# Feed-forward tiles of 512 rows instead of 256, with 512-column first products, in a fused attention and two-feed-forward kernel

## The chip, the cores and the metric

One NeuronCore of a Trainium2 chip runs the whole program. The metric is the device time of one execution in microseconds (us). TensorE (PE) does the matrix products, VectorE (DVE), ScalarE (ACT) and GpSimd (POOL) the elementwise work, and SyncE (SP) issues most transfers.

## The reference

Eight batches of an attention without softmax, with a squared ReLU, feed a feed-forward layer of eight experts (top 1, with rows that skip it), and then a shared feed-forward layer whose activation is a rational function.

```python
# u, v: (8, 3072, 256); z: (8, 3072, 64)
scores = (1 / S) * z @ z.T
x = u * (np.maximum(scores, 0) ** 2 @ v)            # 24576 rows of 256
# experts: w1 (8, 256, 1024), w2 (8, 1024, 256)
do = x @ w_skip > 0
e = argmax(x[do] @ w_gate); gate = softmax(...)[e]
x[do] += gate * (np.maximum(x[do] @ w1[e], 0) @ w2[e])
# shared: w_in (256, 2048), w_out (2048, 256)
h = x @ w_in
g = (a0 + a1*h + a2*h**2 + a3*h**3) / (1 + abs(b0)*abs(h) + abs(b1)*h**2 + 1e-6)
out = g @ w_out
```

## The kernel before

Every product is made three times in the type fp32r, from operands split into a high and a low part (high by high, high by low, low by high).

**Attention** is cut into 1152 *ticks*, each of 256 query rows by 256 key rows: four score products (`S`, L649 and L650, from `T1` and its swapped copy `T4`), ReLU and square on ACT (L653, L656), a split into `ah` (ACT or DVE) and `al` (DVE, L664), and twelve products with `V` into the PSUM bank `accA` (L672). Twelve ticks make a row tile, which is then gated with `u` (`xs`, L731), routed to its expert and scattered to DRAM.

**Feed-forward** work is cut into *tiles* of 256 gathered rows (`mr`), transposed by PE (`mt`, L1090) and split into `mx` (L1095, L1098). A tile runs through *units*, four for an expert tile (kind 1) and eight for a shared tile (kind 2). A unit covers 256 columns of the hidden layer: twelve first products of 256 columns (`h`, L1054, in two halves `l1a` and `l1b`), the activation, and twelve second products (`l2h`, `l2l`, L1065) which add up in the PSUM bank `accM`. The activation of a shared unit is a chain over three engines: `abs` and `p1` on ACT (L1202, L1203), `q0` (L1209) and `q1` (L394), `p2`, `p3` on DVE (L1215, L1216), `ln`, `ex` on ACT (L1217, L1218), `gh`, `v`, `w` on DVE (L1219, L1220, L1222), `gl` (L394). For `q0`, `q1`, `gl` and some splits the planner chooses between DVE, POOL and ACT. After the last unit `mo` takes the sum out of `accM` (ACT, L1117, or DVE, L1112).

**Order.** Batches form five groups of 1, 2, 2, 2, 1. Expert units of a group are followed by its shared units; the attention of the following groups is mixed into the shared units (these stretches are called mixed below). `CARRY` = 1 tile of each group is put off to the next group's shared units. After the last tick come 56 shared units with the last group's 32 expert units (called `n`), and then the last group's 96 shared units alone. The class `Flow` simulates the engines with fixed costs and writes out one order for each engine; `PAR`, `SLIP` and `AHEAD` are its tuned due times and margins. `RINGS` gives the number of buffers of each tile name: of the eight PSUM banks six are called `b` (scores, `h`, transposes; `h` is given back by `w`, `S` by `al`), one is `accA`, one `accM`.

Of the kernel before, what the change touches and what calls it, by code (L numbers as in the profile page):

```python
# [8 lines left out]
F32 = mybir.dt.float32  # L9
F32R = mybir.dt.float32r  # L10
# [38 lines left out]
    "u.a": 4.46, "u.s": 22.81, "u.t": -51.57, "v.x": -18.1, "v.y": -44.71, "w.x": -20.81, "w.y": -12.53, "wsc.w": -0.79,  # L49
    "wsc1.f": 13.53, "wscc.w": -13.79, "wsch.w": -24.06, "wscl.w": 14.97,  # L50
# [3 lines left out]
SLIP = {"P": 7.64, "A": 0.24, "D": 0.96, "G": 27.68, "Q": 9.0}  # L54
# [15 lines left out]
class Flow:  # L70
# [7 lines left out]
    AHEAD = {"P": 35.26, "A": 5.17, "D": 97.38, "G": 8.79, "Q": 0.0}  # L78
# [138 lines left out]
def tile_attn_moe_moe2(  # L217
# [42 lines left out]

    NCH1 = E * FP1
# [10 lines left out]
    ident = sb.tile([P, P], F32, tag="mp", name="ident", bufs=3)  # L272
# [7 lines left out]
    onef = sb.tile([P, P], F32, tag="mu", name="onef", bufs=3)  # L280
# [3 lines left out]
    trif = sb.tile([P, P], F32, tag="mu", name="trif", bufs=3)  # L284
# [73 lines left out]
    def w_raw(n, wa, wb, fp):  # L358

        wide = wa.dtype != F32  # L360
        if wide:
            da = sb.tile([P, 512, 2], I32, tag="W", name=f"wda{n}", bufs=NW)
            db = sb.tile([P, 512, 2], I32, tag="W", name=f"wdb{n}", bufs=NW)
            wa, wb = wa.bitcast(I32), wb.bitcast(I32)
            la, lb, cw = da.rearrange("p c w -> p (c w)"), db.rearrange("p c w -> p (c w)"), 2
        else:
            da = sb.tile([P, 512], F32, tag="wr", name=f"wra{n}", bufs=WR)
            db = sb.tile([P, 512], F32, tag="wr", name=f"wrb{n}", bufs=WR)
            la, lb, cw = da, db, 1
        w_load(la, lb, wa, wb, fp, cw)  # L370
        return da, db

    def w_parts(n, dst, half, raw):
        o = 512 * half
        if raw.dtype == I32:
            r = sb.tile([P, 512], F32, tag="wr", name=f"wr{n}_{half}", bufs=WR)
            for _ in from_f64(r, raw, f"{n}_{half}"):
                pass
            raw = r
# [24 lines left out]
    def tl(tag, name, dt=F32, cols=512):  # L404
        return sb.tile([P, cols], dt, tag=tag, name=name, bufs=RINGS[tag])
# [29 lines left out]
    def put_unit(m, fp, kd):  # L435
        wn = ("v", m.w0 + fp) if kd == "n" else m.w0 + fp
# [9 lines left out]
    def m_tiles(kind, tls, nfp, base, nb):  # L446
        out = []
        for i, (g, idx) in enumerate(tls):
            m = MTile()
            m.kind, m.g, m.idx, m.nfp = kind, g, idx, nfp  # L450
            m.prev = out[-1][0] if out else None
            m.src = (xs_d, x2_d)[kind - 1][g][idx * TT : (idx + 1) * TT, :]
            m.w0 = base + (i // nb) * FP1 if kind == 1 else base
            out += [(m, fp) for fp in range(nfp)]
# [5 lines left out]
    own = [[(g, i) for i in range(nb * NIC)] for g, nb in enumerate(groups)]  # L460
# [7 lines left out]
    for g, nb in enumerate(groups):  # L468
        final = g == NG - 1 and g > 0
        if not final:  # L470
            us = m_tiles(1, [(g, i) for i in range(E * nb)], FP1, base, nb)
# [951 lines left out]
```

## Time and profile before

| | |
|---|---|
| median of 3 runs | 5650.31 us (5645.02 to 5654.39) |
| profiled execution | 5656.78 us |
| its span, first to last instruction | 5654.9 us |
| PE busy | 5462.3 us, 97% |
| DVE busy | 4607.6 us, 81% |
| ACT busy | 4177.9 us, 74% |
| POOL busy | 3151.3 us, 56% |
| granted TensorE clock, mean | 0.993 |

The shares are means over stretches with different limits, so the stretches have to be read apart. Busy time is the time in which at least one instruction of the engine was under way; PE's products overlap (one starts while the one before it drains), so their spacing is read from starts, not from durations.

### The profile page before, as it was taken

To read this page: it belongs to the slowest core of one execution; us is meant where nothing else is said; L and a number is where in the kernel's file an instruction comes from. 1 tells how busy PE (TensorE), PEld (TensorE's weight loads), DVE (VectorE), ACT (ScalarE), POOL (GpSimd) and SP (SyncE) were. 2 spreads that over 40 slices of the span, in tenths; PEclk is the share of its full clock that TensorE was granted. 3 is DMA by queue.
4 is the path that set the end of the run, shared out by engine and by line. 5 is a ranking of instruction groups with operands and counts; after the bars stand their busy time and mean duration, and the time that the engine had idled before them with its cause. 6 is when DMAs were issued, how large, how long until landed. Compare 5 with 4: busy or idle time off the path is not lost.

```text
span 5654.9 us, 119372 instructions
## 1 busy us (share of the span) xinstructions
PE 5462.3 (97%) x45285; PEld 5421.0 (96%) x45285; DVE 4607.6 (81%) x7474; ACT 4177.9 (74%) x7625; POOL 3151.3 (56%) x4456
## 2 busy tenths in 40 slices
PE   9999999999999999999999999999999999999887
PEld 9989999999999999999999999999999999999887
DVE  6765777776379899989539999899837999999999
ACT  8865888886278888888538878888826777765787
POOL 3443455444255565556326666666625777665787
PEclk9999999999999999999999999999999999999999
DMA  4376111114521110011451010001353000035000
GB/s 126 121 261 246 37 44 45 34 37 147 204 72 31 33 54 30 31 31 53 152 207 37 29 53 29 29 26 37 105 188 117 22 26 24 23 123 168 20 20 15
DMA packets 219786, 435.95 MB, mean 77 GB/s; under 512 B 30078, under 2 KB 145257, under 8 KB 197698
## 3 DMA queue, kind: packets, MB, share of 16 engines
q1 hardware_dynamic: 191938, 360.52, 18.9%
q0 software_dynamic: 27264, 67.71, 3.5%
q8 instruction: 358, 5.87, 0.4%
q14 instruction: 226, 1.85, 0.1%
HBM read 291.65 MB, written 153.09 MB: 79 GB/s over the span
## 4 chain that ended last, share of the span: by engine, by line
PE 73%; DVE 14%; issue 5%; POOL 3%; ACT 2%; DMA 2%; DVEq 0%; SPq 0%; POOLq 0%; ACTq 0%
PE accA L672 25%; PE h L1054 18%; PE accM L1065 18%; PE S L649 4%; PE S L650 4%; DVE mq L1220 3%; DVE mgh L1219 2%; DVE mq L1222 2%; DVE mp L1215 2%; POOL mgl L394 1%; DVE h L1216 1%; PE lp L761 1%; DMA wr<-in_moe_w_dram 1%; PE mt L1090 1%; PE xp L747 1%
## 5 line engine op out<-in xcount | busy, mean ns | idle before, releaser
L1054 PE MATMUL h<-mx,W 128*128 128x256 f32 x11904 | 1632.6, 284 | 48.7 <-DVE mq L1222 39.7
L1054 PEld LDWEIGHTS h<-mx,W 128*128 128x128 f32 x11904 | 1510.3, 189 | 59.1 <-issue 23.6
L672 PE MATMUL accA<-V,ah 128*128 128x256 f32 x9216 | 1293.4, 283 | 5.9 <-DVE xs L731 4.2
L394 POOL TENSOR_TENSOR mgl<-mq,mu 128x512 fp32r<-128x512 f32 x645 | 860.7, 1336 | 632.7 <-DVE mq L1222 436.3
L672 PEld LDWEIGHTS accA<-V,ah 128*128 128x128 f32 x9216 | 1182.8, 190 | 7.9 <-DVE xs L731 3.3
L1065 PE MATMUL accM<-W,mgh 128*128 128x256 f32 x7936 | 1125.5, 285 | 36.5 <-ACT mo L1117 19.6
L1065 PEld LDWEIGHTS accM<-W,mgh 128*128 128x128 f32 x7936 | 1025.7, 192 | 44.6 <-ACT mo L1117 24.3
L664 DVE TENSOR_TENSOR al<-S,ah 128x512 fp32r<-128x512 f32 x1152 | 784.8, 682 | 141.9 <-ACT ah L398 127.8
L653 ACT ACTIVATE S<-S 128x512 f32<-128x512 f32 x1152 | 676.0, 587 | 115.8 <-PE S L650 110.3
L1209 POOL TENSOR_SCALAR mq<-mu,coef 128x512 f32<-128x512 f32 x536 | 477.2, 890 | 505.7 <-ACT mu L1202 496.8
L672 PE MATMUL accA<-V,al 128*128 128x256 f32 x4608 | 746.0, 284 | 2.4 <-DVE al L664 2.3
L1202 ACT ACTIVATE mu<-h 128x512 f32<-128x512 f32 x768 | 458.2, 597 | 380.6 <-PE h L1054 271.1
L656 ACT ACTIVATE S<-S 128x512 f32<-128x512 f32 x1152 | 677.3, 588 | 21.9
L1215 DVE TENSOR_TENSOR mp<-mp,h 128x512 f32<-128x512 f32 x768 | 521.3, 679 | 194.6 <-ACT mp L1203 179.1
L1220 DVE SCALAR_TENSOR_TENSOR mq<-mq,mgh 128x512 f32<-128x512 f32 x768 | 671.7, 875 | 10.1
L1065 PE MATMUL accM<-W,mgl 128*128 128x256 f32 x3968 | 647.1, 285 | 30.5 <-POOL mgl L394 26.6
L1217 ACT ACTIVATE mu<-mq 128x512 f32<-128x512 f32 x768 | 484.8, 631 | 227.6 <-POOL mq L394 141.7
L672 PEld LDWEIGHTS accA<-V,al 128*128 128x128 f32 x4608 | 633.2, 191 | 3.4 <-DVE al L664 3.4
L1219 DVE SCALAR_TENSOR_TENSOR mgh<-h,coef,mu 128x512 fp32r<-128x512 f32 x768 | 570.4, 743 | 69.5 <-ACT mu L1218 56.2
L398 ACT ACTIVATE ah<-S 128x512 fp32r<-128x512 f32 x946 | 563.5, 596 | 71.6 <-PE accA L672 57.7
L394 POOL TENSOR_TENSOR mq<-mq,mu 128x512 f32<-128x512 f32 x422 | 562.9, 1334 | 59.0 <-DVE mq L1209 23.6
L650 PE MATMUL S<-T,T 128*128 128x256 f32 x2304 | 593.5, 282 | 0.0
(152 smaller groups left out, 8374.7 us busy)
## 6 DMA issues: line engine op xcount, KB each, us to landing
W<-wsc SPq DMA_DIRECT2D x96, 1024.0 KB, 6.1
wsc<-W SPq DMA_DIRECT2D x32, 1024.0 KB, 8.6
W<-wsc POOLq DMA_DIRECT2D x32, 1024.0 KB, 5.3
Wv<-wsc SPq DMA_DIRECT2D x64, 512.0 KB, 4.7
vr<-in_v_dram SPq DMA_DIRECT2D x96, 256.0 KB, 3.3
xs<-in_u_dram SPq DMA_DIRECT2D x96, 256.0 KB, 2.9
x<-xs SPq DMA_DIRECT2D x96, 256.0 KB, 2.2
mr<-x SPq DMA_DIRECT2D x96, 256.0 KB, 3.3
```

The source lines that it names most:

```text
L394: (nc.vector if e == "D" else nc.gpsimd).tensor_tensor(*a, **k)
L398: act(out, in_, AF.Copy)
L650: mm(o, lhsT=lw, rhs=T4[b, ic], start=False, stop=(jj == 1), skip_group_check=True)
L653: act(st["s"], st["s"], AF.Relu, scale=1.0 / S)
L656: act(st["s"], st["s"], AF.Square)
L664: ttt(st["lo"], st["s"], st["hi"].bitcast(F32), op=ALU.subtract)
L672: mm(accs[b, ic][:, it * TT : (it + 1) * TT], lhsT=a[:, jj * TT + it * P : jj * TT + (it + 1) * P], rhs=VV[b, jp][:, vi, jj * D : (jj + 1) ...
L1054: mm(o, lhsT=lw, rhs=rw, start=(ff == 0 and k == 0 and i == 0), stop=(ff == 1 and k == NK - 1 and i == 2), skip_group_check=True,)
L1065: mm(acc[:, it * TT : (it + 1) * TT], lhsT=(gh, gl)[part][:, c0 : c0 + P], rhs=w[i][:, 512 + ff * D : 512 + (ff + 1) * D], start=(first an ...
L1215: pt("p2", "D.602", ["p1", "abs"], lambda: ttt(s["p"], s["p"], s["h"], op=ALU.mult))
L1219: pt("gh", "D.663", ["ex", "p3"], lambda: stt(buf("mgh", F32R), s["h"], a0, s["u"], op0=ALU.add, op1=ALU.mult), ["mgh"])
L1220: pt("v", "D.602s", ["gh"], lambda: stt(s["q"], s["q"], CQ, s["gh"].bitcast(F32), op0=ALU.add, op1=ALU.mult))
```

## The change

1. **Tiles of 512 rows** (`m_tiles` with `nh` = 2, `plan_half`) for the experts of groups 2 to 4 and for all shared work; the experts of the first and the last group stay at 256. A unit now covers 128 hidden columns of 512 rows: six first products of 512 columns (`mm_l1w`), an activation of the same 128x512 size as before, and twelve second products of 256 columns (`mm_l2w`), six into each of two banks. A tile has twice the units of before, and the number of units stays the same (256 expert units and 768 shared ones). `CARRY` still counts tiles, so that 16 units are put off where 8 were.
2. **Buffers.** `accM` has two banks and `b` five; `mp` goes from 3 to 2 buffers, `T1` from 7 to 6, `mr` from 3 to 4 (of which a tile takes two), `mo` from 1 to 2; `zr` and `xt` now share the ring `wr`; the default rows (`dflt`) are kept in DRAM.
3. **Spacers** of 64 bytes stand before six tile names. In the built program tiles start at these bytes modulo 128. Before: `T1`, `T4`, `V`, `ah`, `al` 64; `W`, `mgh`, `mgl` 0; `mx` 96. Now: `T1`, `V`, `W` 32; `T4`, `ah`, `al`, `mgh`, `mgl`, `mx` 96. The moving and the stationary operand of nearly every product (not of `T1` by `T1`) are 64 bytes apart.
4. **Other due times and margins**, so that the planner writes another order.

```diff
 PAR = {
-    "S.a": 4.89, "S.t": -2.78, "T1.a": -21.74, "T1.s": 3.66, "T1.t": -47.54, "T1hi.a": -75.61, "T1hi.s": -3.79,
...
+    "S.a": 5.12, "S.t": -3.04, "T1.a": -59.25, "T1.s": -0.83, "T1.t": -58.86, "T1hi.a": -74.61, "T1hi.s": -18.49,
...
-SLIP = {"P": 7.64, "A": 0.24, "D": 0.96, "G": 27.68, "Q": 9.0}
+SLIP = {"P": 8.95, "A": 0.25, "D": 24.11, "G": 5.02, "Q": 9.0}
...
-    AHEAD = {"P": 35.26, "A": 5.17, "D": 97.38, "G": 8.79, "Q": 0.0}
+    AHEAD = {"P": 10.76, "A": 4.45, "D": 125.36, "G": 8.71, "Q": 0.0}
...
+    spacers = {"T4": 16, "V": 16, "ah": 16, "W": 16, "mgh": 16, "mx": 16}
+
+    def sbt(shape, dt, tag, **kw):
+        if tag in spacers:
+            sb.tile([P, spacers.pop(tag)], F32, tag="sp" + tag, name="sp" + tag, bufs=1)
+        return sb.tile(shape, dt, tag=tag, **kw)
...
-        "b": 6, "accA": 1, "accM": 1, "ah": 2, "al": 2, "V": NJP, "T1": NZC + 1, "T4": 2,
-        "zr": 1, "xt": 1, "xs": 2, "wr": WR, "W": NW, "mu": 3, "mp": 3, "mq": 3, "mgh": 3, "mgl": 3,
-        "mr": 3, "mx": 2, "mti": 4, "mo": 1,
+        "b": 5, "accA": 1, "accM": 2, "ah": 2, "al": 2, "V": NJP, "T1": NZC, "T4": 2,
+        "xs": 2, "wr": WR, "W": NW, "mu": 3, "mp": 2, "mq": 3, "mgh": 3, "mgl": 3,
+        "mr": 4, "mx": 2, "mti": 4, "mo": 2,
...
-    own = [[(g, i) for i in range(nb * NIC)] for g, nb in enumerate(groups)]
+    own = [[(g, i) for i in range(nb * NIC // 2)] for g, nb in enumerate(groups)]
...
-        us = m_tiles(2, t2s[g], FP2, base - (FP2 if final else 0), nb)
+        us = m_tiles(2, t2s[g], FP2, base - (FP2 if final else 0), 2)
...
+    def mm_l1w(h, w, xh, xl, ff, k):
+
+        c0 = k * TT + ff * P
+        xhk, xlk = xh[:, k * 512 : (k + 1) * 512], xl[:, k * 512 : (k + 1) * 512]
+        wh, wl = w[0][:, c0 : c0 + P], w[1][:, c0 : c0 + P]
+        for i, (lw, rw) in enumerate(((wh, xhk), (wh, xlk), (wl, xhk))):
+            mm(h, lhsT=lw, rhs=rw, start=(k == 0 and i == 0), stop=(k == NK - 1 and i == 2), skip_group_check=True)
+
...
+    def mm_l2w(accs_, w, ff, gh, gl, first, last, part):
+        for it in range(4):
+            for i in (0, 1) if part == 0 else (0,):
+                mm(
+                    accs_[it // 2][:, it % 2 * TT : (it % 2 + 1) * TT], lhsT=(gh, gl)[part][:, it * P : (it + 1) * P],
...
-        return "accA" if m.g == NG - 1 > 0 and (m.kind == 1 or m.idx % 2) else "accM"
+        return "accA" if m.g == NG - 1 > 0 and m.kind == 1 else "accM"
...
-        add(at["l1a"], ("l1a", t), "P.714", lambda: l1(0), after=prev + [("m", m.mi, "lo"), ("W", wn)], takes=[hu])
...
+        pl1 = "P.714" if m.nh == 1 else "P.69"
```

On PE, in a mixed stretch (the fourth batch's attention), first the order before: the first products of shared unit 218, and the second products of earlier units of the same weights' ring.

```order
L672 MATMUL accA3_7_25668<-V3_1_18718,al517_25624 128x256 x4
L1065 MATMUL accM38_25106<-W79_22959,mgh215_25562 128x256 x8
L1054 MATMUL h218_25734<-mx39_25408,W74_22542 128x256 x12
L1065 MATMUL accM38_25106<-W79_22959,mgl215_25613 128x256 x4
```

At the like place the changed program has this.

```order
L684 MATMUL accA3_8_24888<-V3_8_18530,al536_25287 128x256 x4
L1095 MATMUL accM23_0_24320<-W78_22082,mgh220_25225 128x256 x4
L1095 MATMUL accM23_1_24321<-W78_22082,mgh220_25225 128x256 x4
L1095 MATMUL accM23_0_24320<-W78_22082,mgl220_25260 128x256 x2
L1095 MATMUL accM23_1_24321<-W78_22082,mgl220_25260 128x256 x2
L1077 MATMUL h222_25360<-mx23_23910,W79_22281 128x512 x6
```

Twelve first products of 256 columns have become six of 512; the second products are as many and as wide as before, and go to two banks.

On PE, at the change from one shared tile to the next in the last group, the order before (tile 156 has `accM`, tile 157 the bank `accA`, whose buffer is free there; the program's name for both is `accM`):

```order
L1065 MATMUL accM156_78307<-W159_62330,mgh999_78608 128x256 x8
L1054 MATMUL h1004_78656<-mx157_78327,W156_62109 128x256 x12
L1065 MATMUL accM157_78677<-W152_61810,mgh1000_78674 128x256 x8
L1065 MATMUL accM156_78307<-W159_62330,mgl999_78671 128x256 x4
L1054 MATMUL h1005_78706<-mx157_78327,W157_62127 128x256 x12
```

and now, from tile 85 to tile 86:

```order
L1095 MATMUL accM85_0_72082<-W159_58214,mgl991_72660 128x256 x2
L1095 MATMUL accM85_1_72083<-W159_58214,mgl991_72660 128x256 x2
L1095 MATMUL accM86_0_72685<-W152_57472,mgh992_72663 128x256 x4
L1095 MATMUL accM86_1_72686<-W152_57472,mgh992_72663 128x256 x4
L1077 MATMUL h997_72699<-mx86_72222,W154_57652 128x512 x6
```

The new tile's second products used to start before the old tile's had ended, in another bank; now they stand right behind them and need both of its banks emptied first. Such a place comes half as often.

## Rows read from the trace of the kernel before

**Rows 1.** Windows: span, busy us (x count) of each engine, granted clock, DMA share, GB/s.

```profile
core 0: us, PE busy (x) PEld busy (x) DVE busy (x) ACT busy (x) POOL busy (x), PEclk, DMA share, GB/s
330.00:540.00 210.00, 183.61 (x1415) 180.15 (x1414) 112.56 (x198) 112.79 (x214) 64.82 (x120) 0.92 0.78 290
540.00:4270.00 3730.00, 3698.33 (x31052) 3688.41 (x31052) 2932.74 (x4879) 2760.38 (x5134) 1978.11 (x3037) 1.00 0.21 70
4270.00:5000.00 730.00, 691.24 (x5695) 684.43 (x5694) 704.19 (x1062) 555.12 (x981) 507.33 (x583) 0.99 0.12 38
5000.00:5290.00 290.00, 270.26 (x2192) 265.86 (x2192) 272.44 (x377) 179.16 (x295) 167.90 (x161) 0.98 0.41 136
5290.00:5655.00 365.00, 297.31 (x2274) 281.73 (x2272) 351.24 (x491) 291.43 (x453) 292.55 (x221) 0.97 0.06 17
```

**Rows 2.** Windows: the second and third mixed stretch.

```profile
1560.00:2720.00 1160.00, 1152.36 (x9695) 1150.96 (x9694) 1041.74 (x1717) 962.38 (x1787) 682.32 (x988) 1.00 0.13 42
2930.00:4050.00 1120.00, 1107.91 (x9289) 1102.12 (x9288) 1014.33 (x1649) 906.74 (x1669) 709.68 (x978) 1.00 0.13 42
```

**Rows 3.** Waits of PE, 540 to 4270: us in total, times, longest us.

```profile
PE S L649 <- DVE mq L1222: 4.8, 4, 1.4
...
PE h L1054 <- DVE al L664: 3.2, 3, 1.2
```

**Rows 4.** Waits of PE, 4270 to 5000, largest two.

```profile
PE xp L747 <- DVE xs L731: 18.1, 9, 2.2
PE accM L1065 <- ACT mo L1117: 15.7, 13, 1.7
```

**Rows 5.** Waits of PE, 5290 to 5655, the largest.

```profile
PE h L1054 <- DVE mq L1222: 37.1, 39, 1.6
```

**Rows 6.** Windows of line L1054 alone (PE, PEld).

```profile
540.00:4270.00 3730.00, 1077.92 (x7827) 992.58 (x7827) 1.00 0.21 70
```

**Rows 7.** The chain that ended last: start us, us, what.

```profile
1157.17 4.31 PE accA L672 x36
...
1576.40 4.32 PE h L1054 x36
```

**Rows 8.** Timeline of PE near 314: start us, us, what.

```profile
314.68 0.46 PE L570 MATMUL tp<-ident_r,zh 128*128 128x128 f32 x4
314.98 0.35 PE L649 MATMUL S<-T,T 128*128 128x256 f32 x1
```

**Rows 9.** Timeline of PE near 2976.

```profile
2976.13 1.11 PE L672 MATMUL accA<-V,ah 128*128 128x256 f32 x8
2977.07 0.64 PE L672 MATMUL accA<-V,al 128*128 128x256 f32 x4
```

**Rows 10.** Lines of DVE, 4270 to 5000: count | busy us, mean ns | idle before.

```profile
L1220 DVE SCALAR_TENSOR_TENSOR mq<-mq,mgh 128x512 f32<-128x512 f32 x146 | 143.9, 986 | 0.8
L1216 DVE SCALAR_TENSOR_TENSOR h<-mp,coef,h 128x512 f32<-128x512 f32 x147 | 108.6, 744 | 0.6
L1222 DVE SCALAR_TENSOR_TENSOR mq<-h,coef,mq 128x512 f32<-128x512 f32 x146 | 108.3, 742 | 1.5
L1219 DVE SCALAR_TENSOR_TENSOR mgh<-h,coef,mu 128x512 fp32r<-128x512 f32 x146 | 107.9, 739 | 0.0
L1215 DVE TENSOR_TENSOR mp<-mp,h 128x512 f32<-128x512 f32 x147 | 99.2, 675 | 0.5 <-ACT mp L1203 0.5
...
L394 DVE TENSOR_TENSOR mq<-mq,mu 128x512 f32<-128x512 f32 x45 | 33.5, 744 | 0.7
L394 DVE TENSOR_TENSOR mgl<-mq,mu 128x512 fp32r<-128x512 f32 x28 | 30.7, 1097 | 1.1
```

**Rows 11.** Lines of ACT, whole span.

```profile
L1117 ACT ACTIVATE mo<-accM 128x512 f32<-128x512 f32 x96 | 57.2, 595 | 20.8 <-PE accM L1065 19.5 <-DVE mq L1220 0.8
```

More of the change, by code (lines that the diff above doesn't have):

```diff
@@ L375, in w_parts @@
         if raw.dtype == I32:
-            r = sb.tile([P, 512], F32, tag="wr", name=f"wr{n}_{half}", bufs=WR)
+            r = sbt([P, 512], F32, tag="wr", name=f"wr{n}_{half}", bufs=WR)
             for _ in from_f64(r, raw, f"{n}_{half}"):
@@ L504, in tile_attn_moe_moe2 @@
             done, nt, span = len(x_tick), NA - len(x_tick), len(us) - POST
-            ms = m_tiles(1, [(NG - 1, i) for i in range(E * groups[-1])], FP1, 0, groups[-1])
-            lo, hi = span + TAIL, len(us) - CARRY * FP2
+            ms = m_tiles(1, [(NG - 1, i) for i in range(E)], FP1, 0, 1)
+            lo, hi = span + TAIL, len(us) - CARRY * 2 * FP2
             k = 0
@@ L629, in load @@
             b, ic = row // NIC, row % NIC
-            ut[row] = sb.tile([P, 2, RW], F32, tag="xs", name=f"xs{row}", bufs=RINGS["xs"])
+            ut[row] = sbt([P, 2, RW], F32, tag="xs", name=f"xs{row}", bufs=RINGS["xs"])
             nc.sync.dma_start(out=ut[row][:, :, 0:D], in_=rows4(u[b], 0, ic))
@@ L743, in r1 @@
             xp = R["xp"] = bank("b", f"xp{nm}")
+            R["xt"] = tl("wr", f"xt{nm}")
             for t in range(2):
@@ L752, in r2 @@
         def r2():
-            R["xt"] = sb.tile([P, 512], F32, tag="xt", name=f"xt{nm}", bufs=1)
             act(R["xt"], R["xp"], AF.Copy)
@@ L975, in load @@
             if v:
-                wt_t[n] = [sb.tile([P, 1024], F32R, tag="V", name=f"Wv{i}_{c}", bufs=NJP) for i in range(2)]
+                wt_t[n] = [sbt([P, 1024], F32R, tag="V", name=f"Wv{i}_{c}", bufs=NJP) for i in range(2)]
                 for i in range(2):
@@ L1070, in mm_l2, with plan_half @@
                         )
+    def mm_l2w(accs_, w, ff, gh, gl, first, last, part):
[3 more added lines that the diff above has]
+                    accs_[it // 2][:, it % 2 * TT : (it % 2 + 1) * TT], lhsT=(gh, gl)[part][:, it * P : (it + 1) * P],
+                    rhs=w[i][:, 512 + ff * D : 512 + (ff + 1) * D],
+                    start=(first and part == 0 and it % 2 + i == 0),
+                    stop=(last and part == 1 and it % 2 == 1), skip_group_check=True,
+                )
     def acc_tag(m):
-        return "accA" if m.g == NG - 1 > 0 and (m.kind == 1 or m.idx % 2) else "accM"
+        return "accA" if m.g == NG - 1 > 0 and m.kind == 1 else "accM"
     def plan_tile(m):
+        for h in range(m.nh):
+            plan_half(m, h)
+    def plan_half(m, h):
         mi = m.mi
-        k = ("m", mi)
+        k = ("m", mi, h)
+        st = {}
+        end = m.nh - 1
         def load():
-            m.rows = sb.tile([P, 2, RW], F32, tag="mr", name=f"mr{mi}", bufs=RINGS["mr"])
+            m.rows[h] = sbt([P, 2, RW], F32, tag="mr", name=f"mr{mi}_{h}", bufs=RINGS["mr"])
             w = RW if m.kind == 1 else D
-            nc.sync.dma_start(out=m.rows[:, :, 0:w], in_=m.src.rearrange("(p t) c -> p t c", t=2))
+            nc.sync.dma_start(out=m.rows[h][:, :, 0:w], in_=m.srcs[h].rearrange("(p t) c -> p t c", t=2))
         def tr():
-            m.tp = bank("b", f"mt{mi}")
+            st["tp"] = bank("b", f"mt{mi}_{h}")
+            if h == 0:
+                n = 512 * m.nh
+                mx = sbt([P, 2 * n if xb == "V" else 2048], F32R, tag=xb, name=f"mx{mi}", bufs=RINGS[xb])
+                m.xh, m.xl = mx[:, 0:n], mx[:, n : 2 * n]
             for t in range(2):
@@ L1165, in plan_unit @@
         at = {o: xu + d for o, d in LAG[kd].items()}
-        wn = ("v", m.w0 + fp) if kd == "n" else m.w0 + fp
-        first, last = fp == 0, fp == m.nfp - 1
+        wn = ("v", m.w0 + fp) if kd == "n" else m.w0 + fp // m.nh
+        first, last, ff = fp == 0, fp == m.nfp - 1, fp % 2
         hu = ("b", ("u", t))
@@ L1172, in l1 @@
                 s["h"] = bank("b", f"h{t}")
-            mm_l1(s["h"], wt_t[wn], m.xh, m.xl, (half,))
+            if m.nh == 1:
+                mm_l1(s["h"], wt_t[wn], m.xh, m.xl, (half,))
+            else:
+                mm_l1w(s["h"], wt_t[wn], m.xh, m.xl, ff, half)
         def l2(part):
             if first and part == 0:
-                m.acc = bank(acc_tag(m), f"accM{m.mi}")
-            mm_l2(m.acc, wt_t[wn], s["gh"], s["gl"] if part else None, first, last, (part,))
+                m.acc = [bank(acc_tag(m), f"accM{m.mi}_{h}") for h in range(m.nh)]
+            if m.nh == 1:
+                mm_l2(m.acc[0], wt_t[wn], s["gh"], s["gl"] if part else None, first, last, (part,))
+            else:
+                mm_l2w(m.acc, wt_t[wn], ff, s["gh"], s["gl"] if part else None, first, last, part)
         def buf(tag, dt=F32):
@@ L1190, in plan_unit @@
         prev = [("l1a", t - 1)] if t else []
-        add(at["l1a"], ("l1a", t), "P.714", lambda: l1(0), after=prev + [("m", m.mi, "lo"), ("W", wn)], takes=[hu])
-        add(at["l1b"], ("l1b", t), "P.714", lambda: l1(1), after=[("l1a", t)], frees=[("V" if kd == "n" else "mx", ("mx", m.mi))] if last else [])
+        pl1 = "P.714" if m.nh == 1 else "P.69"
+        add(at["l1a"], ("l1a", t), pl1, lambda: l1(0), after=prev + [("m", m.mi, h, "lo") for h in range(m.nh)] + [("W", wn)], takes=[hu])
+        add(at["l1b"], ("l1b", t), pl1, lambda: l1(1), after=[("l1a", t)], frees=[("V" if kd == "n" else "mx", ("mx", m.mi))] if last else [])
         if m.kind == 1:
@@ L1227, in plan_unit @@
             at["l2h"], ("l2h", t), "P.952", lambda: l2(0), after=[("gh", t)] + ([("l2l", m.ts[fp - 1])] if fp else []),
-            takes=[(acc_tag(m), ("m", m.mi))] if first else [],
+            takes=[(acc_tag(m), ("m", m.mi, h)) for h in range(m.nh)] if first else [],
         )
@@ L1324, in overflow_tile @@
                 )
-        oi = sb.tile(o1, I32, tag="oi", name=f"oi{e}")
+        oi = sbt(o1, I32, tag="oi", name=f"oi{e}")
         nc.vector.tensor_copy(oi, tk)
```

207 lines of the change are left out of this document (110 added, 97 removed), and 35 rows, old and new, of the table PAR.

## The prediction

> **What bounds the kernel now.** I read the table of stretches first, since the busy shares of the page are means over stretches of different kinds. From 540 to 4270 us PE is busy 3698 of 3730 us, 99.1%, at a granted clock of 1.00 (2.4 GHz), and starts 31052 products [rows 1], one per 120.1 ns. There is almost nothing to win there but in PE's own work. From 4270 to 5000 DVE is busy 704 of 730 us, 96.5%, and PE only 691; from 5000 to 5290 DVE 94% and PE 93%; from 5290 on DVE 351 of 365 us, 96%, and PE 81% [rows 1]. These last 1385 us go by DVE. From 330 to 540 the transfers bind (DMA share 0.78, clock 0.92 [rows 1]); its expert tiles stay at 256 rows. The two long mixed stretches are nearly balanced: DVE at 1042 of 1160 and 1014 of 1120 us, 90% and 91%, while PE idles 8 and 12 us [rows 2].
>
> Next I read who makes PE wait. From 540 to 4270 the waits for DVE to give back a PSUM bank are small: 4.8 us for `w` to free an `h`, 3.2 us for `al` to free an `S` [rows 3]. From 4270 to 5000 PE waits 18.1 us for the gating of a row and 15.7 us, 13 times, for `mo` to empty `accM` [rows 4]. At the end 37.1 us are waits for an `h` bank [rows 5]: units queue up before DVE.
>
> Last I read the spacing of products. The chain shows runs of 36 without a break, attention's `V` by `ah` in 4.31 us and first products in 4.32 us: 120 ns each, whatever the product [rows 7].
>
> **The change, part by part.**
>
> *First products.* 7827 of them lie between 540 and 4270 [rows 6], 3914 pairs. The change moves eight shared units out of this stretch (below), so 3914 - 48 = 3866 pairs become single products of 512 columns. The trace has no product of 512 columns. If the cost goes by columns, one takes 240 ns and nothing is saved. The nearest row on the other side are four products of 128 columns in 0.30 us, 75 ns each [rows 8]: 128 columns more cost 45 ns there, which gives 120 + 2 x 45 = 210 ns for 512, a saving of 30 ns. One row at each side is no reason to lean, so I take the middle, 225 ns: 3866 x 15 = **-58 us** (ends 0 and -116). In the last 1385 us the same saving falls on PE while DVE binds, and I count nothing.
>
> *The units put off.* `CARRY` = 1 is now a tile of 16 units. The first mixed stretch has 80 shared units for 88, with the same attention; the stretch from 4270 has 152 for 144. Eight units leave a stretch that PE binds: 8 x 24 products x 120 ns = **-23 us**. They come where DVE binds. A unit has five steps on DVE, 986 + 744 + 742 + 739 + 675 ns = 3.89 us [rows 10], so 31 us. Counted by unit in the two orders, `q1` stands on DVE there 58 times for 45 (13 x 744 ns = +9.7) and `gl` 20 for 28 (8 x 1097 ns = -8.8) [rows 10]. That is +32 us of DVE's time; a little goes into its 26 idle us, so **+30 us**.
>
> *5000 to 5290.* `q1` on DVE 19 times for 29, `gl` 6 for 3: -7.4 + 3.3, **-4 us** at the same durations. The experts of the last group are unchanged.
>
> *Operands 64 bytes apart.* 31052 - 7827 = 23225 other products in the PE-bound stretch keep their shape. Before, `V` and `ah` start at the same byte modulo 128, and `mx` and `W` 96 bytes apart; both run at 120 ns [rows 7]. That says that 0 and 96 are equal, and nothing on 64. The quickest run of eight takes 0.94 us, 117.5 ns [rows 9]. So the effect lies between 0 and 2.5 ns, and with no row nearer to either I take about half, 1.2 ns: **-28 us** (ends 0 and -58).
>
> What the rows show there may be set against the Trainium skill. Products of 256 columns stand 120 ns apart [rows 7]. "TensorE: Matmul & The Clock Gate", section "Back-to-back issue gap", gives columns / 2.4 + 2.5 ns for an isolated gap, so 109 and 216 ns. The trace disagrees with the first by 11 ns, and the section itself says that a stream with weight loads is set by both; by its formula a pair would save only 2.5 ns, and the term above would be -10 us for -58 (an estimate from that page). The same page, section "Step-by-step: what each phase is for", says that PE reads moving and stationary operands through two independent ports, so that loading the next weights takes no read bandwidth from a running product. By that rule the spacing is worth nothing; no run of before has operands 64 bytes apart to test it.
>
> *DVE in the mixed stretches.* A quicker PE brings DVE nearer to its limit. In the third mixed stretch `q1` moves to DVE in 31 more units (122 for 91): 1014 + 31 x 744 ns = 1037 us. With its share of the savings, (58 + 28) x 1120 / 3730 = 26 us, the stretch would be 1094 us and DVE at 95%. At 90% PE loses about 1% [rows 2], at 96.5% 5.3% [rows 1], so here some 3.5%, or 27 us more than now; in the second stretch (92%) 11. If the planner's order absorbs it, nothing. The middle: **+19 us** (0 to +38).
>
> *Tile ends.* A 512-row tile needs both `accM` banks, so the next tile's second products wait for two evictions of 595 ns [rows 11]. Between 540 and 4270 other products stand in the gap. In the last group, where tiles used to alternate between `accM` and `accA`, there are five such ends: 6 us if nothing hides them, 0 if DVE goes on working from the queue, so **+3 us**.
>
> *At nothing:* `zr` and `xt` in the ring `wr`, one buffer less of `mp` and `T1`, the default rows from DRAM. What hides them is PE's queue of attention and `h` work; the one place with little cover is 330 to 540, where weights pass through `wr` and PE already idles 26 of 210 us [rows 1]. If the cover is gone there, I allow +10 us.
>
> **The sum.** -58 - 23 + 30 - 4 - 28 + 19 + 3 = -61 us. The profiled execution took 5656.8 us, its span 5654.9; the median of the runs is 5650.3, 6.5 below. 5650.3 - 61 = **5589 us**.
>
> **Rivals.**
>
> *Both effects at their good ends.* 24 ns for a pair and 2.5 ns for every other product: -93 - 58 - 23 + 30 - 4 + 3, and DVE's push-back in full (+38), is -107: 5543 us. For it: the 75 ns of 128 columns. Against it: those four may owe it to something that 512 columns don't have, and the balanced stretches let little through.
>
> *The change does not do what it says.* A column costs what it costs, and the bytes don't matter: 0 - 23 + 30 - 4 + 3 + about 5 of push-back = +11, 5661 us. (The Trainium skill's page "TensorE: Matmul & The Clock Gate", in the two sections named above, speaks for this case; with its 2.5 ns for a pair the estimate is 5651.) For it: every product row reads 120 ns, whatever its operands [rows 7]. Against it: the 128-column row.
>
> *Five banks are too few: slower.* `b` loses a sixth of its banks, so PE can run less far ahead of DVE, and the products queued behind a first product that waits for a bank wait with it. Now such waits are about 8 us of 3730 [rows 3]. What it looks like when banks run out is seen at the end: 37.1 of 365 us, 10% [rows 5]. At a quarter of that rate between 540 and 4270 it costs 95 us: 5684. It decides against the change from 61 us on, 1.6% of the stretch. For it: six banks are all held at the end, and one tile name fewer can be in flight. Against it: PE's waits there are near nothing with six, and at the end itself DVE binds, so that a shorter queue costs little as long as DVE always has a unit.
>
> **How the numbers follow.** The forecast has 0.52, both good ends 0.22, nothing gained 0.13, five banks 0.13. The likeliest case alone reaches from 5565 to 5625. To leave out no more than 2 in 10 the range goes to 5525, under the 5543 of the good case, and up to 5660, the time of the case without effect. The good ends of all terms together (-116 - 58 - 23 + 30 - 4 = -171) would give 5479, which I leave out. A measurement tells a change of 0.2% (11 us) from none: faster holds the first two cases and a little of the third, 0.77; same 0.10; slower 0.13.
>
> **What the profile after would show.** If the first term is right, runs of first products start 225 ns apart (210 to 240), and the stretch up to the last group's experts is shorter by about 90 us. If the spacing counts, runs of attention's products go below 119 ns. If the units put off count, the stretch before the last tick grows by some 30 us with DVE at 97% or more. If the banks are too few, PE's waits for `w` and `al` in the mixed stretches go from 8 us to 60 or more. The end should stay at 365 us within 10. The prediction is wrong if first products come 240 ns apart with nothing else gained, if bank waits eat the saving, or if products of both kinds quicken by more than I allow and DVE lets it through.

## The result and the profile after

| | before | after |
|---|---|---|
| median, run side by side on one chip | 5651.38 us, 4 runs (5645.02 to 5654.39) | 5579.86 us, 4 runs (5577.05 to 5585.14) |
| ratio after / before | | 0.9876 [0.9859, 0.9893] |
| span of the profiled execution | 5654.9 us | 5575.3 us |

The change is 71.5 us faster; 61 us were predicted. The page of after, its span and the first engines:

```profile
span 5575.3 us, 107018 instructions
PE 5362.4 (96%) x39525; PEld 5027.9 (90%) x39525; DVE 4533.8 (81%) x7470; ACT 4202.2 (75%) x7663; POOL 3090.5 (55%) x4422
```

The windows of after answer to [rows 1]:

```profile
core 0: us, PE busy (x) PEld busy (x) DVE busy (x) ACT busy (x) POOL busy (x), PEclk, DMA share, GB/s
330.00:540.00 210.00, 187.99 (x1506) 183.50 (x1506) 121.56 (x218) 123.44 (x233) 65.98 (x133) 0.97 0.77 282
540.00:4200.00 3660.00, 3619.92 (x27058) 3422.55 (x27057) 2882.63 (x4844) 2777.20 (x5135) 1870.46 (x2947) 1.00 0.22 73
4200.00:4930.00 730.00, 693.29 (x4794) 635.00 (x4793) 702.50 (x1106) 595.81 (x1049) 528.21 (x592) 0.99 0.10 34
4930.00:5215.00 285.00, 261.65 (x1814) 237.64 (x1812) 255.51 (x362) 170.64 (x282) 180.62 (x167) 0.99 0.40 133
5215.00:5576.00 361.00, 283.32 (x1670) 235.84 (x1670) 337.46 (x469) 253.77 (x405) 304.97 (x248) 0.96 0.05 16
```

The two long windows do not end at the same work: that of after ends with the first shared unit behind the fourth group's experts (ACT starts on it at 4200.4), that of before 28 us ahead of it (4298.2). From 540 to that unit the stretch bound by PE is 98 us shorter, and PE is still busy for 99% of it. The chain of waits shows why: runs of attention's products by `ah`, and first products (columns: start us, us, what), to set against [rows 7].

```profile
1007.71 4.10 PE accA L684 x36
...
1012.75 1.42 PE h L1077 x6
...
1031.95 1.39 PE h L1077 x6
...
1048.47 2.83 PE accA L684 x24
```

Thirty-six products of unchanged shape take 4.10 us for 4.31, 114 ns each for 120, and another run of 24 takes 2.83 us, 118 ns each. Six products of 512 columns take 1.39 and 1.42 us, 232 and 237 ns each, where a pair of 256 took 240. By all starts in the trace from 540 to 4200, half of the products of `V` by `ah` follow the one before within 117 ns (120 before), and half of the first products of 512 columns within 232. The window of line L1077 alone answers to [rows 6]:

```profile
540.00:4200.00 3660.00, 1044.08 (x3918) 681.15 (x3918) 1.00 0.22 73
```

That is 266.5 ns of busy time for a product, and 1077.92 / 3913.5 = 275.4 ns for a pair before: 9 ns. The shorter run in the chain gives 8, the longer one 3, so I take 8 to 9 ns for a pair.

PE's waits of after, 540 to 4200 (first fence) and 5215 to 5576 (second):

```profile
PE mt L1130 <- DMA mr<-xs: 16.7, 20, 1.9
...
PE h L1077 <- DVE mq L1277: 1.6, 4, 0.6
```

```profile
PE h L1077 <- DVE mq L1277: 39.2, 50, 2.1
```

Waits for DVE to give back a bank did not grow in the long stretch [rows 3], and at the end they stand about where they stood [rows 5]. What is new is the first row: the rows `mr` of an expert tile arrive late.

To follow the sum through the program I use three starts in the trace: of the first `abs` (ACT, `mu` for `h`) of all, of the first `abs` behind the fourth group's experts (there the fourth group's shared units begin), and of the last one.

| us | first unit | fourth group's shared units | last unit | between the last two |
|---|---|---|---|---|
| before | 522.2 | 4298.2 | 5636.0 | 1337.8 |
| after | 511.1 | 4200.4 | 5555.6 | 1355.2 |
| changed, no spacers | 520.9 | 4270.0 | 5628.0 | 1358.0 |
| before, with spacers | 509.6 | 4235.4 | 5572.6 | 1337.2 |
| before, 16 units put off | 520.3 | 4276.1 | 5624.2 | 1348.1 |

98 us are gained up to the fourth group's shared units, and 17 given back after that. The profiled executions of before and after differ by 80 us, the medians by 71.5, so the parts read from them add up to some 8 us too much.

### The profile page after: what moved, and what is told of

The parts are those of the page before. It is cut to its first block, busy times and chain, and to the rows that moved or that the text cites. A ratio compares the mean times of both kernels' runs of the same rounds, so it can differ in the third digit from the quotient of the medians.

```text
span 5575.3 us, 107018 instructions
## 1 busy us (share of the span) xinstructions
PE 5362.4 (96%) x39525; PEld 5027.9 (90%) x39525; DVE 4533.8 (81%) x7470; ACT 4202.2 (75%) x7663; POOL 3090.5 (55%) x4422
## 4 chain that ended last, share of the span: by engine, by line
PE 70%; DVE 13%; ACT 6%; DMA 4%; issue 4%; POOL 3%; SPq 0%; DVEq 0%; ACTq 0%; POOLq 0%
PE accA L684 24%; PE h L1077 17%; PE accM L1095 16%; PE S L661 4%; PE S L662 4%; DVE mq L1275 3%; DVE mgh L1274 3%; DMA mr<-xs 2%; DVE h L1271 2%; DVE mq L1277 2%; DVE mp L1270 1%; PE lp L773 1%; PE mt L1130 1%; ACT mp L1258 1%; ACT mu L1272 1%
## 5 line engine op out<-in xcount | busy, mean ns | idle before, releaser
L1077 PE MATMUL h<-mx,W 128*128 128x512 f32 x5760 | 1540.7, 400 | 64.1 <-DVE mq L1277 58.9
L405 POOL TENSOR_TENSOR mgl<-mq,mu 128x512 fp32r<-128x512 f32 x655 | 892.1, 1363 | 692.9 <-DVE mq L1277 395.8
L1077 PEld LDWEIGHTS h<-mx,W 128*128 128x128 f32 x5760 | 1013.5, 190 | 250.6 <-DVE mq L1277 75.3
L1095 PE MATMUL accM<-W,mgh 128*128 128x256 f32 x7680 | 1054.5, 280 | 10.6 <-DVE mgh L1274 6.6
L1095 PEld LDWEIGHTS accM<-W,mgh 128*128 128x128 f32 x7680 | 979.6, 189 | 32.3 <-DVE mgh L1274 8.9
L409 ACT ACTIVATE ah<-S 128x512 fp32r<-128x512 f32 x996 | 594.9, 598 | 63.3 <-PE accA L684 41.7
L1095 PE MATMUL accM<-W,mgl 128*128 128x256 f32 x3840 | 615.1, 282 | 27.9 <-POOL mgl L405 27.3
L1275 DVE SCALAR_TENSOR_TENSOR mq<-mq,mgh 128x512 f32<-128x512 f32 x768 | 617.4, 805 | 15.7 <-DVE mgh L1274 0.5
L1258 ACT ACTIVATE mp<-h,coef 128x512 f32<-128x512 f32 x768 | 595.5, 775 | 23.3 <-DVE h L1271 18.8
L1095 PEld LDWEIGHTS accM<-W,mgl 128*128 128x128 f32 x3840 | 537.3, 189 | 63.4 <-POOL mgl L405 39.7
```

What stands on the lines that cost most here:

```text
L405: (nc.vector if e == "D" else nc.gpsimd).tensor_tensor(*a, **k)
L409: act(out, in_, AF.Copy)
L1077: mm(h, lhsT=lw, rhs=rw, start=(k == 0 and i == 0), stop=(k == NK - 1 and i == 2), skip_group_check=True)
L1095: mm(accs_[it // 2][:, it % 2 * TT : (it % 2 + 1) * TT], lhsT=(gh, gl)[part][:, it * P : (it + 1) * P], rhs=w[i][:, 512 + ff * D : 512 + ( ...
L1258: pt("p1", "A.664", ["l1b"], lambda: act(buf("mp"), s["h"], AF.Identity, scale=a3, bias=a2), ["mp"])
L1275: pt("v", "D.602s", ["gh"], lambda: stt(s["q"], s["q"], CQ, s["gh"].bitcast(F32), op0=ALU.add, op1=ALU.mult))
```

## The experiments

**The spacers alone.** First the change without them:

```diff
-    spacers = {"T4": 16, "V": 16, "ah": 16, "W": 16, "mgh": 16, "mx": 16}
+    spacers = {}
```

> The changed kernel without its spacers: the order of all engines is the same. T1, T4, V, W, ah, al, mgh and mgl then all start at byte 32 modulo 128, mx stays 64 bytes from W, so that first products keep the distance of 64 and attention's and second products lose it. Theory 1 (the distance makes narrow products quicker): attention's and second products come 120 ns apart instead of 116 to 118, and the time rises by 2.5 ns x some 23000 products of the stretch that PE binds, 45 to 65 us, to 5625 to 5645 us. Theory 2 (the distance is nothing, the planner's new order or the buffers brought what the width did not): no change, 5580 within 10.

5646.32 us, ratio to before 0.9987 [0.9978, 0.9997] over 10 runs. The chain has attention's products at 120 ns again, while first products keep their 233 ns:

```profile
1027.87 4.32 PE accA L684 x36
...
1033.15 1.40 PE h L1077 x6
```

Then the kernel before, its tiles and order untouched, with spacers that put `T1`, `V`, `W` on byte 64 and `T4`, `ah`, `al`, `mgh`, `mgl`, `mx` on byte 0 (modulo 128):

```diff
+    spacers = {"T4": 16, "mgh": 16, "mx": 8}
```

> The kernel before with three spacers, nothing else: T1, V, W start at byte 64, T4, ah, al, mgh, mgl, mx at byte 0 modulo 128. Theory 1 (distance counts by itself): narrow products, the first products among them, go from 120 to 117 or 118 ns, 31000 x 2 to 2.6 ns, 50 to 75 us faster, 5575 to 5600, less what DVE pushes back. Theory 2 (it counts only with the wide tiles' order): same as before, 5650 within 10.

5598.92 us, ratio 0.9903 [0.9887, 0.992]. A run of the chain there (accA is L681 in this kernel):

```profile
1054.91 3.66 PE accA L681 x32
```

114 ns again. So the spacers are worth 54 us in the old kernel and 66 us in the new (63 by the two ratios): most of the gain, with nothing else of the change. Here and below, differences from the change are between medians that were not taken side by side; by the ratios to before they come out 2 to 4 us smaller.

**The width alone.** The change with each first product split into two of 256 columns:

```diff
-            mm(h, lhsT=lw, rhs=rw, start=(k == 0 and i == 0), stop=(k == NK - 1 and i == 2), skip_group_check=True)
+            for c in range(2):
+                mm(
+                    h[:, c * TT : (c + 1) * TT], lhsT=lw, rhs=rw[:, c * TT : (c + 1) * TT],
...
```

> The changed kernel with each first product of 512 columns issued as two of 256 with the same weights; order, buffers and spacers as in the change. Theory 1 (the width saves about what the changed trace shows, 232 ns against twice 117 to 120): 3 to 9 ns for each of some 3900 pairs in the stretch that PE binds, 10 to 35 us slower, 5590 to 5615. Theory 2 (the width was the gain, 15 ns a pair, as I put it): 55 us or more slower, 5635 and up.

5590.2 us, ratio 0.9888 [0.9872, 0.9905]. That is 10 us above the change, and the two intervals overlap. With the spacers a pair of 256 columns is cheaper too, which leaves the width little to save. The window of the first products (L1078 here) says how little:

```profile
540.00:4200.00 3660.00, 1043.74 (x7789) 966.93 (x7790) 1.00 0.22 72
```

A pair takes 268.0 ns of busy time, a product of 512 columns in the change 266.5: 1.5 ns, or 6 us over the stretch.

**The units put off.**

```diff
-LEAD, TAIL, POST, CARRY, MROW = 24, 8, 56, 1, 8
+LEAD, TAIL, POST, CARRY, MROW = 24, 8, 56, 2, 8
```

> The kernel before with CARRY = 2, so that 16 units are put off as in the change, and the planner orders them anew with due times tuned for 8. Theory 1 (eight units move from where PE binds to where DVE binds): the first mixed stretch gets 23 us shorter, the one from 4270 some 30 longer, 5650 to 5665 in all. Rival (the put-off units fill waits there, or the first stretch's gain is larger than what they cost later): 5630 to 5645.

5649.92 us, ratio 0.9993 [0.9983, 1.0002] over 10 runs: no difference. By the table above 22 us are gained before the fourth group's shared units and 10 are lost from there on, in the one execution profiled.

**TensorE alone.** A kernel that leaves out the whole computation (its output is zeros) and runs 64 products at a time on zeros, with the two operands 0 to 192 bytes apart (beyond a multiple of 256):

```python
nc.tensor.matmul(o[:, 0:cols], lhsT=wt[:, w0 + c : w0 + c + P], rhs=mov[:, m : m + cols], start=(i == 0), stop=(i == n - 1))
```

> None of the computation, only TensorE: runs of 64 fp32r products of 128, 256 and 512 columns on zeros, with the stationary operand 0, 16, 32, 64, 96, 128 or 192 bytes (modulo 128) from the moving one, no other engine at work. Theory 1 (PE's own two reads get in each other's way when they start in the same half of 128 bytes): 256 columns take about 120 ns at 0 and 128 bytes and 113 to 117 at 64 and 192; 512 columns about 230, with little difference. Theory 2 (the other engines' reads of the memory are the cause, and the distance only changes when they meet): no difference by distance here, and all runs at one spacing.

The timeline (start us, us, what); a run's spacing is the distance to the next row's start divided by 64. `n` has 256 columns, `w` 512, `s` has 128. The ends zero, q, quarter, half, threeq, whole, onehalf are 0, 16, 32, 64, 96, 128 and 192 bytes; `base` moves both operands by 32, `fix` repeats one and the same product.

```profile
56.52 7.31 PE L36 MATMUL shalf<-mov,wt 128*128 128x128 f32 x64
63.66 7.31 PE L36 MATMUL sthreeq<-mov,wt 128*128 128x128 f32 x64
...
85.10 7.88 PE L36 MATMUL nzero<-mov,wt 128*128 128x256 f32 x64
92.82 7.74 PE L36 MATMUL nq<-mov,wt 128*128 128x256 f32 x64
...
107.97 7.42 PE L36 MATMUL nhalf<-mov,wt 128*128 128x256 f32 x64
115.22 7.84 PE L36 MATMUL nthreeq<-mov,wt 128*128 128x256 f32 x64
122.91 7.75 PE L36 MATMUL nwhole<-mov,wt 128*128 128x256 f32 x64
130.49 7.70 PE L36 MATMUL nonehalf<-mov,wt 128*128 128x256 f32 x64
138.03 14.72 PE L36 MATMUL wzero<-mov,wt 128*128 128x512 f32 x64
152.59 14.68 PE L36 MATMUL wq<-mov,wt 128*128 128x512 f32 x64
167.10 15.09 PE L36 MATMUL wquarter<-mov,wt 128*128 128x512 f32 x64
182.03 15.10 PE L36 MATMUL whalf<-mov,wt 128*128 128x512 f32 x64
196.96 15.15 PE L36 MATMUL wthreeq<-mov,wt 128*128 128x512 f32 x64
211.94 15.04 PE L36 MATMUL wwhole<-mov,wt 128*128 128x512 f32 x64
226.82 14.82 PE L36 MATMUL wonehalf<-mov,wt 128*128 128x512 f32 x64
241.47 7.82 PE L36 MATMUL nfixzero<-mov,wt 128*128 128x256 f32 x64
...
308.34 7.70 PE L36 MATMUL nbasehalf<-mov,wt 128*128 128x256 f32 x64
315.88 15.10 PE L36 MATMUL wbasehalf<-mov,wt 128*128 128x512 f32 x64
```

256 columns take (92.82 - 85.10) / 64 = 120.6 ns at distance 0 and 113.3 at 64 (`nhalf`); but the other three runs with operands 64 bytes apart modulo 128 (`nonehalf`, `nfixhalf`, `nbasehalf`) take 117.8. 512 columns go the other way round, 227.5 at 0 and 233.3 at 64. The distance modulo 128 does not settle their time either: 128 bytes apart (`wwhole`) they take 232.5 ns and not 227.5, 192 bytes apart (`wonehalf`) 228.9 and not 233.3. No other engine computes in these runs, and from 85 us on the transfers have ended too (DMA share 0.01 at most): the spacing goes by where PE's own two operands lie. Why it does so is not shown.

**First products at distance 0.** That run called for a kernel in which `mx` stands on the byte of `W` (modulo 128); the order of instructions is that of the change.

```diff
-    spacers = {"T4": 16, "V": 16, "ah": 16, "W": 16, "mgh": 16, "mx": 16}
+    spacers = {"T4": 16, "V": 16, "ah": 16, "W": 16, "mgh": 16, "mq": 16}
```

> The changed kernel with the moving rows of first products (mx) 0 bytes instead of 64 from the weights W (modulo 128); all other operands stay 64 bytes apart, the order of instructions is the same. Theory (TensorE's own two reads disturb each other, and the best distance depends on the width: in the run of products alone 512 columns took 227 ns at distance 0 and 233 at 64, 256 columns the other way round, 120.6 and 113.3): first products of 512 columns come 227 ns apart instead of 232, some 3900 of them in the stretch bound by TensorE, so 15 to 25 us faster than the changed kernel, 5555 to 5565 us; the start, where tiles of 256 rows have these operands too, loses up to 5 us. Rival (64 bytes is the better distance for every product in the full kernel, and the run alone misses what the other engines do): first products go to 240 ns, 20 to 30 us slower than the changed kernel, 5600 to 5610 us.

5587.68 us, ratio 0.9887 [0.9871, 0.9904]: 8 us above the change, with overlapping intervals, and neither theory. Of the 8 us 5 are lost before the first unit (516.1 for 511.1), where tiles of 256 rows have these operands too. The window of its first products reads

```profile
540.00:4200.00 3660.00, 1040.76 (x3909) 680.22 (x3909) 1.00 0.22 73
```

266.2 ns each for 266.5. In the whole kernel 512 columns cost the same at both distances. But 227 ns was the wrong run to compare with: the built program has `W` 128 bytes from `mx` beyond a multiple of 256, as in `wwhole`, and that run took 232.5 ns, as much as the kernel's first products. To see whether the other engines' traffic takes the 6 ns away, as I supposed then, the products alone were run again, first by themselves and then (names with `d`) while DVE adds and ACT copies tiles in SBUF.

> Leaves out the whole computation (the output is zeros). Runs of 64 products of 256 and of 512 columns with operands 0, 16 and 64 bytes apart (modulo 128), first with TensorE alone, then the same again while VectorE adds and ScalarE copies tiles of 512 columns in SBUF without a break (names that begin with d). Theory (what lengthens a first product at distance 0 in the whole kernel, 232 ns for 227 alone, is the SBUF traffic of the other engines): alone 120.6 and 113.3 ns at 0 and 64 bytes with 256 columns, 227 and 233 with 512; under the traffic 512 columns at 0 go to about 232 ns, and at 64 stay at 233. Rival (the traffic is not it; it is the sequence of tiles or the data): every run under the traffic is within 1 ns of the same run alone.

```profile
35.41 7.84 PE L38 MATMUL nzero<-mov,wt 128*128 128x256 f32 x64
43.08 14.70 PE L38 MATMUL wzero<-mov,wt 128*128 128x512 f32 x64
57.62 7.74 PE L38 MATMUL nq<-mov,wt 128*128 128x256 f32 x64
...
79.69 7.70 PE L38 MATMUL nhalf<-mov,wt 128*128 128x256 f32 x64
87.23 15.10 PE L38 MATMUL whalf<-mov,wt 128*128 128x512 f32 x64
...
106.72 7.83 PE L38 MATMUL dnzero<-mov,wt 128*128 128x256 f32 x64
114.39 14.70 PE L38 MATMUL dwzero<-mov,wt 128*128 128x512 f32 x64
128.92 7.74 PE L38 MATMUL dnq<-mov,wt 128*128 128x256 f32 x64
...
151.00 7.70 PE L38 MATMUL dnhalf<-mov,wt 128*128 128x256 f32 x64
158.54 15.10 PE L38 MATMUL dwhalf<-mov,wt 128*128 128x512 f32 x64
```

At distance 0 256 columns take 119.8 ns and 512 take 227.2 alone, 119.8 and 227.0 under the traffic; at 64 bytes 256 columns take 117.8 ns both times. The rival holds: this traffic (SBUF reads and writes of DVE and ACT) changes nothing. Nor do transfers: the first two runs had those that write the output beside them, at 416 to 420 GB/s, and agree with the first kernel's, which had none, within 1 ns. By `wwhole` there may be no 6 ns left to explain. That the distance modulo 256 is the rule is not shown, though: in the change without spacers `W` lies 192 bytes from `mx`, where products alone took 228.9 ns (`wonehalf`), and first products came 233 ns apart.

**Five banks, and the tables.** The kernel before with five `b` banks, planned anew from its own tables:

```diff
-        "b": 6, "accA": 1, "accM": 1,
+        "b": 5, "accA": 1, "accM": 1,
```

> The kernel before with five b banks for six (the eighth bank is unused), ordered anew by the planner with due times tuned for six. Theory 1 (five are enough in the mixed stretches, and the end goes by DVE): no more than 15 us slower, 5650 to 5665. Rival (five banks are too few): PE's waits for w and al between 540 and 4270 grow from 8 to 60 us or more, 5700 and up.

5808.7 us, ratio 1.0267 [1.025, 1.0284]: 153 us slower than before, where I expected at most 15. So with tables tuned for six a bank is worth much in that kernel, but not by the sign the rival had: PE's waits for `w` and `al` to give back a bank are 2.7 us from 540 to 4300. The change has five and is faster, and what differs is the tiles, the second `accM` bank and the tables. The next kernel takes the change and gives it the old tables:

```diff
-SLIP = {"P": 8.95, "A": 0.25, "D": 24.11, "G": 5.02, "Q": 9.0}
+SLIP = {"P": 7.64, "A": 0.24, "D": 0.96, "G": 27.68, "Q": 9.0}
...
-    AHEAD = {"P": 10.76, "A": 4.45, "D": 125.36, "G": 8.71, "Q": 0.0}
+    AHEAD = {"P": 35.26, "A": 5.17, "D": 97.38, "G": 8.79, "Q": 0.0}
```

> The changed kernel with the three tables of numbers that set the order (PAR, SLIP, AHEAD) as before; the tiles, the banks and the spacing are those of the change. Theory A (five banks cost much only with an order tuned for six; the tables of the change absorb it): slower than the changed kernel by 50 us or more, with bank waits of TensorE for mgh, w, al well above those of the changed kernel. Theory B (five banks cost little with tiles of 512 rows, since a pair of first products now holds its two banks for one product and not for two, and the tables are worth little): within 20 us of the changed kernel, 5560 to 5600 us.

5709.55 us, ratio 1.01 [1.0083, 1.0117]: 130 us slower than the change. The last of the three gives the old kernel the new tables:

```diff
-SLIP = {"P": 7.64, "A": 0.24, "D": 0.96, "G": 27.68, "Q": 9.0}
+SLIP = {"P": 8.95, "A": 0.25, "D": 24.11, "G": 5.02, "Q": 9.0}
...
-    AHEAD = {"P": 35.26, "A": 5.17, "D": 97.38, "G": 8.79, "Q": 0.0}
+    AHEAD = {"P": 10.76, "A": 4.45, "D": 125.36, "G": 8.71, "Q": 0.0}
```

> The kernel before, with its six banks, with the three tables of numbers that set the order (PAR, SLIP, AHEAD) taken from the change, and nothing else of it. Theory (each set of tables suits only its own tiles and banks, which is why old tables cost the changed kernel 130 us): 50 to 150 us slower than before, 5700 to 5800 us. Rival (the tables of the change are better for any number of banks, and a part of the gain of 72 us is theirs): faster than before, 5600 to 5640 us.

5725.15 us, ratio 1.013 [1.0113, 1.0147]: 71 us slower than before. Each set of tables suits its own kernel, and there is no gain of the tables by themselves. The largest wait of PE in each, first old kernel with five banks, then change with old tables (both from 540 to 4300), then old kernel with new tables (540 to 4379):

```profile
PE accM L1065 <- DVE mgh L1219: 27.1, 23, 2.7
```

```profile
PE accM L1094 <- DVE mgh L1273: 17.9, 17, 2.8
```

```profile
PE accM L1066 <- DVE mo L1113: 52.6, 20, 6.2
```

In the first two PE comes to a second product before its activation is done; in the third it waits for `mo` to empty the only `accM`, 2.6 us each time, in an order that was made for two. These waits are less than the whole loss. A good part is lost before the first unit, which starts at 570.7, 547.8 and 549.1 us in the three (522.2 before, 511.1 in the change). In the first two, PE begins only 2430 and 2457 products by 330 us (before: 2667, the change: 2692):

```profile
0.00:330.00 330.00, 299.33 (x2430) 298.03 (x2431) 219.23 (x437) 251.44 (x497) 126.74 (x307) 0.96 0.36 116
```

```profile
0.00:330.00 330.00, 293.49 (x2457) 290.72 (x2458) 220.99 (x442) 254.70 (x505) 120.48 (x306) 0.95 0.37 118
```

**The late rows.** In the timeline of the change one of the new waits reads

```profile
1388.21 0.66 PE L1130 MATMUL mt<-ident_r,mr 128*128 128x128 f32 x4 [0.85 <-DMA mr<-xs]
```

Its load was issued at 1382.75, 0.56 us after the second scatter of the tile two before (1382.19), and `mo` had read that tile's buffer by 1376.2. On SP's queue three loads of weights stand right before it, until 1382.65, so in this order it could not have left much earlier, whenever its buffer came free:

```profile
1370.83 11.82 SPq L993 DMA_DIRECT2D W<-wsc  x3
1382.75 0.37 SPq L1119 DMA_DIRECT2D mr<-xs  x1
```

To test the buffer, I gave it back when `mo` is computed:

```diff
-            takes=[("mo", (mi, h))], frees=[(acc_tag(m), k)],
+            after=[("l2l", m.ts[-1])] + ([k + ("ti",)] if m.kind == 1 else []),
+            takes=[("mo", (mi, h))], frees=[(acc_tag(m), k)] + ([("mr", (mi, h))] if m.kind == 1 else []),
...
-                frees=[("mo", (mi, h)), ("mr", (mi, h)), ("mti", (mi, h))],
+                frees=[("mo", (mi, h)), ("mti", (mi, h))],
```

> The changed kernel with a row buffer mr given back when mo has been computed from it, and not only after the second scatter; the order is planned anew from the same tables. In the changed kernel TensorE waits 16.7 us, 20 times, for the rows of an expert tile (mt for mr), whose load stands after the scatter of the tile two before. Theory A (the ring of four row buffers is what makes the rows late): these waits go to under 5 us and the kernel is 8 to 15 us faster than the changed kernel, 5565 to 5572 us. Theory B (the loads are late because they queue behind loads of weights that wait for second products; the ring is not it): the waits stay at 12 us or more and the time within 8 us. Against both: if a new order costs anything by itself, the waits fall and the time does not.

5613.93 us, ratio 0.993 [0.9913, 0.9946]: 34 us slower than the change, 10 of them before the first unit (520.8 for 511.1). The waits doubled, and on SP's queue the loads of rows (L1119) now wait for `mo` 40 times for 10 in the change, 89.1 us for 73.9:

```profile
PE mt L1130 <- DMA mr<-xs: 35.1, 32, 2.5
```

```profile
SPq L1119 <- DVE mo L1153: 89.1, 40, 27.9
```

In the new order the loads wait for `mo` to give back the buffer, and the rows come to PE no earlier. Theory A is wrong about the remedy; B foresaw that the waits stay, not that the kernel slows by 34 us. Whether the queue or the new order makes the rows late was not told apart.

## Why the prediction was right, and which of its terms were off

The total (-61 for -71.5) and its mechanism, a PE-bound stretch that shrinks because products come closer, held: -58 - 23 - 28 + 19 gave 90 us for that stretch, and 98 are gained up to the fourth group's shared units. That the total came out so near is luck in part. The two terms on the spacing of products were off by about a factor of two in opposite directions, and the smaller of them was the main gain.

*First products: mis-sized.* The term had 15 ns for a pair; the trace of after shows 8 to 9, and the spacers would have given a part of that to pairs of 256 columns as well. 3866 pairs at 8.5 ns are 33 us for the 58 predicted; beside the spacers the width is worth only 6 us by the window and 10 by the medians. The error lies in its choice of the middle between 210 and 240 ns. The row for 210 was one group of four products of 128 columns, 75 ns apart, and 128 columns more were taken to cost 45 ns. In the products-alone kernel 128 columns take (63.66 - 56.52) / 64 = 111.6 ns at a distance of 64 bytes, 2 ns less than 256 columns in the quickest run there; 512 take twice as long as 256. So the step from 128 to 256 says nothing of that from 256 to 512. The trace of before had a warning: its `mt`, also products of 128 columns, come 109 ns apart (median of 297 distances from 540 to 4200).

*Operands 64 bytes apart: mis-sized the other way.* The term had 1.2 ns a product, -28 us, with -58 as its good end. Measured are 54 us (old kernel) and 66 us (new), part of it outside the stretch: the first unit starts 10 to 13 us earlier in both kernels with spacers. In the new kernel 60 us of it lie between the first unit and the fourth group's shared units, 2.6 ns for each of 23225 products; runs in the chain lie between 114 and 118 ns for 120. The rule weighed there, two independent read ports, so that a weight load takes nothing from a running product ("TensorE: Matmul & The Clock Gate", section "Step-by-step: what each phase is for", of the Trainium skill), would make the spacing worth nothing. The products alone disagree: 120.6 ns at 0 bytes against 113.3 or 117.8 at 64 for the same 64 products.

*The units put off.* -23 in the PE-bound stretch was right: 4298.2 to 4276.1 in the old kernel with 16 units. The +30 in the next stretch was too much. From its first `abs` to the last ReLU of a score, the change takes 684.7 us for 675.0, 10 us more; the whole remainder is 10 us longer in the old kernel with 16 units and 17 in the change, for the +29 that -4, +30 and +3 make.

*DVE in the mixed stretches.* The +19 did not come: bank waits did not grow: 1.6 us for `w` to free an `h`, with about 8 us in all before [rows 3]. In their place stands a wait that the prediction did not have, 16.7 us for the rows of expert tiles. It more than makes up PE's increase in idle time: 3660 - 3619.9 = 40 us for 31.7 before [rows 1].

By the runs, the gain up to the fourth group's shared units is then 70 us from the spacers (4270.0 to 4200.4), 22 from the units put off if they are worth in the new kernel what they are in the old, and 6 from all the rest. The width's 33 us and the 17 us of late rows are in that rest; what else takes 10 us in it no run separates. With 17 given back the sum is -81, for the 80 us between the profiled executions.

*The rivals.* Both good ends: true of the spacing, false of the pair. "Nothing gained" fell with the chain at 114 and 232 ns. Five banks: its row, bank waits of 60 us or more, did not appear in the change. Its cost is real, though: with tables tuned for six, five banks cost the old kernel 153 us. The mechanism is not shown: bank waits stayed at 2.7 us there. The prediction gave the new tables no term of their own; with the old tables the change loses 130 us and comes out 56 us slower than before.

## What to carry to other kernels

Where PE is busy for 99% of a long stretch, look at the start-to-start time of equal products: 2.6 ns on 23000 of them was most of the gain here, and spacers alone brought three quarters of it to the old kernel. Test the distance between moving and stationary operands for each shape, in the kernel itself, and compare with a run alone at the same addresses: the distance modulo 128 did not say what 512 columns take. A change of buffers or banks is worth what its own tuned order makes of it; swapping only the tables cost 71 and 130 us.

## What was not expected of the hardware

- With TensorE alone, the bytes at which the two operands stand change the spacing of 256-column products from 113.3 to 120.6 ns and of 512-column products from 226.7 (16 bytes) to 234 ns (96 bytes), in opposite orders at 0 and 64 bytes; 128 columns stay at 111 to 112 ns.
- The distance is not all of it. At 64 bytes 256 columns took 117.8 ns in the second products-alone kernel, (87.23 - 79.69) / 64, and in the first one as well when both operands were moved by 32 bytes, (315.88 - 308.34) / 64. The second kernel's run and the 113.3 ns run issue the same products on the same addresses. In the change both levels occur: of the distances between products of `V` by `ah` from 540 to 4200, 38% are 112 to 115 ns and 55% are 116 to 119 (before: 4% and 41%). What decides between the two was not found.
- The gap formula weighed in the prediction ("TensorE: Matmul & The Clock Gate", section "Back-to-back issue gap", of the Trainium skill), 109 and 216 ns, lies 4 and 11 ns below the best that any run of 64 products showed with fp32r weights, 113.3 and 226.7 ns.
- SBUF traffic of DVE and ACT, each busy 95% of the time, lengthened no product by more than 0.2 ns.
